# Converting the double-precision weights of a fused attention and MLP kernel a block at a time

## The chip, the cores and the metric

The kernel runs on one core of a Trainium2 chip. Its metric is the device time of one execution in microseconds, from the first to the last of the core's work; lower is better. The kernel before takes 1224.53 us (median of three runs, 1223.8 to 1225.92).

## The reference

Eight batches of eight heads, 576 tokens each, go through causal attention with a decay, and the result through an MLP. Cut to what matters:

```python
# q, k, v: (8, 8, 576, 64) float32, f: (8, 8, 576) float32
scores = q @ k.T / 8 + (cum[:, None] - cum[None, :])      # cum = cumsum(log(clip(f)))
attn = exp(scores - max) / (sum + 1e-9)                   # causal rows
x = (attn @ v), heads side by side                        # (4608, 512)
h = x @ w_in                                              # w_in (512, 2048), float64
g = where(h >= 1, h, where(h <= -1, 0, (h + 1) ** 2 / 4))
out = g @ w_out                                           # w_out (2048, 512), float64
```

Both weight matrices arrive as 64-bit floats, 8 MB each. [...]

## The kernel before, in words

**Attention.** The work is cut into 36 jobs of two heads (a "pair") of one batch; batch 0 is cut into two parts, so that it has eight jobs. A job loads q, k and v, makes scores on PE (L470), the decay with its causal mask on GpSimd, called POOL here (L476, L480), the sum of both with its running minimum on DVE (L559), the exponential on ACT (L563), the normalised weights on ACT and DVE (L577, L583, or a transpose through PE, L490 to L512, in the first five jobs), and the product with v on PE (L532, L603).

**MLP.** Tokens go in chunks of 256, features in eight blocks of 256 (NB = 8). A unit is one chunk and one block: 24 or more matmuls against w_in (L645), three passes on ACT and two on DVE (L654 to L659), twelve matmuls against w_out (L673). Numbers are carried as a high and a low half of 16 bits each, hence three products instead of one. Units are woven between the steps of the attention jobs, as many as have their tokens and their weights.

**Weights.** Block i needs 256 columns of w_in (half-step n = 2i) and 256 rows of w_out (n = 2i + 1). `weight_load` brings the raw words of one half-step as two transfers of 512 KB into two raw places; the list RAW names them. There are 21: the 17 tiles `place0` to `place16` that the halves go to later, and two halves each of `early` and `x1`, two activation buffers that the start leaves free. `weight_split(n)` then works on one half-step, on each of its two parts of 512 elements by itself:

- DVE makes single-precision words by three integer operations (L195, L198, L201; the scratch is the tile `u`, which the MLP units use too);
- a bound of the magnitude is taken per partition: by a maximum on DVE for w_in (L211), by a sum of magnitudes on ACT for w_out (L215, whose elementwise result goes to a place that is not needed yet); L216 joins the two parts;
- `across` makes one number of the 128 partitions by a transpose and a product on PE (L120, L130) with four small DVE operations around them (L122, L123, L127, L131), and `scale_of` a power of two from it by three more (L108, L102, L110);
- ACT writes the high half (L222); POOL (w_in, L224 and L225) or DVE (w_out, L227) writes the low half.

CONVERT says how many half-steps each of the jobs 3 to 7 takes in; after each of them `load_weights` issues further loads, up to AHEAD = 4 half-steps on, as long as their raw place isn't one that waits to be converted.

**Order.** A scheduler sets the order on each engine when the kernel is built, and each engine runs its list strictly in that order. All loads, and the transposes made by DMA from job 5 on, go through one queue, SP. When an instruction waits, everything behind it on its engine or queue waits too.

Of the kernel before, what the change touches and what calls it, by code (L numbers as in the profile page):

```python
# [8 lines left out]
F32 = mybir.dt.float32  # L9
# [6 lines left out]
P = 128  # L16
# [16 lines left out]

EARLY = ((0, 0, 3), (0, 3, 6), (0, 6, 8))

CONVERT = {3: 3, 4: 3, 5: 4, 6: 4, 7: 2}
LOADS = {0: 2, 1: 3, 2: 4}
AHEAD = 4

RAW = (  # L40
    (1, 2), (3, 4), (5, 6), (7, 8), (9, 10), (11, 12), (16, 17), (18, 19),
    (20, 13), (14, 15), (11, 12), (16, 17), (18, 19), (20, 14), (15, 16), (17, 18),
)


@with_exitstack
def kernel(
# [58 lines left out]
    def scale_of(scale, power, m):  # L106

        nc.vector.tensor_scalar(out=power, in0=m, scalar1=1.0 / TOP, scalar2=None, op0=ALU.mult)  # L108
        even_pow2(power, power)
        nc.vector.reciprocal(scale, power)  # L110

    def across(dst, m):

        n = m.shape[1]
        pt = ps.tile([P, 512], F32, name="s")
        nc.tensor.transpose(pt[0:n, 0:P], m, ident)  # L120
# [10 lines left out]
        nc.vector.tensor_copy(dst, pt[:, P:P + n])  # L131
# [33 lines left out]

    place = [const.tile([P, 2, 2 * DM], F16, name=f"place{i}") for i in range(2 * NB + 1)]
    slots = [t.rearrange("p l c -> p (l c)").bitcast(I32) for t in place] + [r.bitcast(I32) for r in (early[:, 2 * DM:4 * DM], early[:, 0:2 * DM], x1[:, 0:2 * DM], x1[:, 2 * DM:4 * DM])]
    wi = [place[2 * i].rearrange("p l (t c) -> p l t c", t=NKT) for i in range(NB)]  # L170
    wo = [place[2 * i + 1].rearrange("p l (t c) -> p l t c", t=2) for i in range(NB)]
    mi = const.tile([P, NB], F32, name="mi")
    mp = const.tile([P, 2, NB], F32, name="mp")
    sw = const.tile([P, 2, NB], F32, name="sw")

    def weight_load(n):
        i, j = divmod(n, 2)
        if j == 0:
            src = w_in.bitcast(I32)[:, i * 4 * P:(i + 1) * 4 * P].rearrange("(t p) c -> p t c", p=P)
        else:  # L180
            src = w_out.bitcast(I32)[i * 2 * P:(i + 1) * 2 * P, :].rearrange("(t p) c -> p t c", p=P)
        n = src.shape[1] // 2
        for k_, slot in enumerate(RAW[2 * i + j]):
            nc.sync.dma_start(
                slots[slot].rearrange("p (t c) -> p t c", t=n), src[:, n * k_:n * (k_ + 1), :]
            )

    def weight_split(n):
        i, j = divmod(n, 2)
        parts = []  # L190
        for k_, slot in enumerate(RAW[n]):
            top = slots[slot][:, 1::2]
            low = slots[slot][:, 0::2]
            bits = two.tile([P, DM], F32, name="u").bitcast(I32)
            nc.vector.tensor_scalar(  # L195
                out=bits, in0=top, scalar1=0x07FFFFFF, scalar2=3, op0=ALU.bitwise_and, op1=ALU.logical_shift_left
            )
            nc.vector.scalar_tensor_tensor(  # L198
                out=bits, in0=low, scalar=29, in1=bits, op0=ALU.logical_shift_right, op1=ALU.bitwise_or
            )  # L200
# [3 lines left out]
            parts.append((top.bitcast(F32), slice(k_ * DM, (k_ + 1) * DM)))
        hi = place[n][:, 0]
        lo = place[n][:, 1]
        m1 = tiny.tile([P, 1], F32, name="m1", bufs=2)
        ms = tiny.tile([P, 2], F32, name="ms", bufs=2)
        for k_, (wf, c) in enumerate(parts):
            if j == 0:  # L210
                nc.vector.tensor_reduce(  # L211
                    out=ms[:, k_:k_ + 1], in_=wf, axis=AX.X, op=ALU.max, apply_absolute_value=True
                )
            else:
                nc.scalar.activation(lo[:, c], wf, AF.Abs, accum_out=ms[:, k_:k_ + 1])  # L215
        nc.vector.tensor_reduce(out=m1, in_=ms, axis=AX.X, op=ALU.max)  # L216
        m = mi[:, i:i + 1] if j == 0 else tiny.tile([P, 1], F32, name="m2")
        across(m, m1)
        s = sw[:, j, i:i + 1]
        scale_of(s, mp[:, j, i:i + 1], m)  # L220
        for wf, c in parts:
            nc.scalar.activation(hi[:, c], wf, AF.Copy, scale=s)  # L222
            if n % 2 == 0:
                nc.gpsimd.tensor_scalar(out=wf, in0=wf, scalar1=s, scalar2=0.0, op0=ALU.mult, op1=ALU.add)  # L224
                nc.gpsimd.tensor_tensor(out=lo[:, c], in0=wf, in1=hi[:, c], op=ALU.subtract)  # L225
# [519 lines left out]
    for p in range(njobs + 1):  # L745
        w = pairs[p] if p < njobs else None
        nxt = pairs[p + 1] if p + 1 < njobs else None
        steps = []
        if w:
            if w.b not in xs:  # L750
                xs[w.b] = xpool.tile([P, NPAIR, 2, S], F16, name="x")
            if p + 2 < njobs:
                pairs.append(load(p + 2))
            if nxt:
                load_decay(nxt, 0)
                prepare(nxt)
            scores(w, w.r0)

            def step(r):
                if r + 1 < w.r1:  # L760
                    scores(w, r + 1)
                if r == w.r1 - 2 and nxt:
                    load_decay(nxt, 1)
                    if nxt.hp == 0 and nxt.r0 == 0:
                        value_scale(nxt.b)
                    split_values(nxt)
                weights(w, r)
                if r == w.r1 - 1 and p + 2 < njobs:
                    measure(pairs[p + 2])

            steps = [lambda r=r: step(r) for r in range(w.r0, w.r1)]
        if p > 0:
            wp = pairs[p - 1]

            def finish():
                nonlocal tokens
                (early_values if wp.p < NPE else values)(wp, xs[wp.b])
                if wp.hp == NPAIR - 1:
                    if wp.b and wp.r0 == 0:
                        join_scales(wp.b - 1)  # L780
                    tokens = wp.b * S + wp.s1

            steps.insert(4 if len(steps) == NT5 else 2, finish)
        load_weights(LOADS.get(p, 0))
        blocks = CONVERT.get(p, 0)
        quota = -(-ready() // (NPAIR - (p + NPAIR - 1) % NPAIR))
        before, wbefore = done, nw
        for i, st in enumerate(steps):
            st()
            while nw - wbefore < blocks * (i + 1) // len(steps):  # L790
                weight_step()
            while ready() and done - before < quota * (i + 1) // len(steps):
# [39 lines left out]
```

## Time and profile before

| | |
|---|---|
| median of three runs | 1224.53 us |
| profiled execution: its time, its span | 1223.2 us, 1221.4 us |
| busy over the span: PE, DVE, ACT, POOL | 92%, 70%, 62%, 36% |
| weight operations: first and last start | 19.5 us (L195), 200.4 us (L227) |
| weight loads on SP | 32 of 512 KB |

The span is cut into stretches below: the weights are converted in the first 215 us, and PE is close to full from 400 us on. A time in a row of groups is the sum of the durations, and durations of neighbouring instructions overlap a little: how far apart two of them start is read from the timeline.

### The profile page before, as it was taken

What the parts mean: (1) busy time and instruction counts of PE and PEld (TensorE: products, weight loads), DVE (VectorE), ACT (ScalarE), POOL (GpSimd) and SP (SyncE); (2) the same over time, 40 slices, a digit from 0 to 9 for tenths busy, and PEclk for the clock granted to TensorE, in tenths of its full rate; (3) what the DMA queues carried; (4) which work ended last, traced back from release to release, by engine and by line L of the source; (5) the groups of instructions that cost most, each with busy time, mean ns of one, the idle gap of its engine ahead of it and who ended that gap; (6) DMA issues with size and microseconds to landing.
All of it is one profiled execution on the core that took longest, in us unless ns stands there. A gap on an engine that the chain in (4) does not pass through costs nothing.

```text
span 1221.4 us, 24896 instructions
## 1 busy us (share of the span) xinstructions
PE 1118.6 (92%) x8865; PEld 683.2 (56%) x8865; DVE 854.6 (70%) x2423; ACT 762.5 (62%) x1558; POOL 443.9 (36%) x695
## 2 busy tenths in 40 slices
PE   5587677996799999999999999989999999999998
PEld 3354334553456565565655665655665566567665
DVE  6889888776877787777666767777877796522222
ACT  3574665774756676757666667666767687644443
POOL 4758644542633254334333224432443263100000
PEclk9878788899699999999999999999999999999999
DMA  8957543768866768657636736666966685300000
GB/s 230 278 149 199 135 123 79 138 126 175 172 129 140 146 131 162 126 120 141 126 88 134 150 69 126 140 138 123 172 123 135 143 154 114 72 24 2 18 19 18
DMA packets 408541, 152.21 MB, mean 125 GB/s; under 512 B 384225, under 2 KB 385249, under 8 KB 408417
## 3 DMA queue, kind: packets, MB, share of 16 engines
q1 hardware_dynamic: 408416, 150.63, 57.7%
q8 instruction: 69, 1.13, 0.4%
q14 instruction: 56, 0.45, 0.1%
HBM read 75.64 MB, written 9.58 MB: 70 GB/s over the span
## 4 chain that ended last, share of the span: by engine, by line
PE 38%; DVE 5%; DMA 3%; issue 2%; SPq 2%; ACT 2%; POOL 0%; DVEq 0%; ACTq 0%
PE ph L645 16%; PE po L673 16%; PE s L470 3%; PE big L603 2%; DMA ck<-in_v_dram 1%; DVE pr L583 1%; DVE sdr L559 1%; SPq L332 1%; DMA qk<-in_k_dram 1%; PE big L470 1%; DMA qk<-in_q_dram 1%; DVE u L656 1%; DVE g L659 1%; SPq L429 0%; ACT pr L577 0%
## 5 line engine op out<-in xcount | busy, mean ns | idle before, releaser
L645 PE MATMUL ph<-x,place 128*128 128x256 f16 (+3 forms) x4608 | 449.9, 250 | 12.6 <-DVE u L656 7.9
L673 PE MATMUL po<-place,g 128*128 128x512 f16 x1728 | 423.7, 384 | 9.4 <-DVE g L659 5.8
L645 PEld LDWEIGHTS <-place 128*128 128x128 f16 x4608 | 356.0, 99 | 115.2 <-issue 44.8
L673 PEld LDWEIGHTS <-g 128*128 128x128 f16 x1728 | 161.3, 99 | 184.8 <-issue 21.1
L476 POOL TENSOR_SCALAR sdr<-ck,nsig,cqs 128x128 f32<-128x128 f32 (+1 forms) x192 | 155.9, 815 | 229.8 <-DVE pr L583 218.1
L563 ACT ACTIVATE sdr<-sdr,nm 128x384 f32<-128x384 f32 (+1 forms) x248 | 138.5, 559 | 95.1 <-DVE nm L559 84.8
L470 PE MATMUL s<-qkT 64*128 64x384 f16 (+6 forms) x704 | 158.9, 359 | 23.3 <-DVE nm L559 21.6
L656 DVE SCALAR_TENSOR_TENSOR u<-ph,z,u 128x512 f32<-128x512 f32 x136 | 101.6, 747 | 108.8 <-ACT u L655 108.2
L654 ACT ACTIVATE u<-ph,z 128x512 f32<-128x512 f32 x136 | 104.7, 769 | 111.3 <-PE ph L645 110.6
L658 ACT ACTIVATE g<-u,z 128x512 f16<-128x512 f32 x136 | 97.7, 718 | 90.8 <-DVE u L656 90.2
L577 ACT ACTIVATE pr<-sdr,rc 128x384 f16<-128x384 f32 (+1 forms) x236 | 120.0, 556 | 38.7 <-DVE rc L574 16.9
L583 DVE SCALAR_TENSOR_TENSOR pr<-sdr,rc,pr 128x384 f16<-128x384 f32 (+2 forms) x232 | 126.3, 573 | 25.4 <-ACT pr L577 24.2
L476 POOL TENSOR_SCALAR sd<-ck,nsig,cqs 64x576 f32<-64x576 f32 x48 | 54.2, 1130 | 242.6 <-ACT qs L403 91.0
L659 DVE SCALAR_TENSOR_TENSOR g<-u,z,g 128x512 f16<-128x512 f32 x136 | 103.6, 761 | 38.4 <-ACT g L658 38.2
L559 DVE CUSTOM_DVE_ANT_0 sdr<-s,sdr,nalpha 128x128 f32<-128x128 f32 (+1 forms) x192 | 103.2, 545 | 23.1 <-PE s L470 17.0
L470 PEld LDWEIGHTS <-qkT 64*128 64x128 f16 (+1 forms) x864 | 47.9, 99 | 88.0 <-issue 66.5
L480 POOL TENSOR_SCALAR_AFFINE_SELECT sdr<-sdr 128x128 f32<-128x128 f32 x248 | 92.2, 381 | 10.9
L655 ACT ACTIVATE u<-u 128x512 f32<-128x512 f32 x144 | 89.8, 623 | 2.5
L603 PE MATMUL big<-pT,vs 128*64 128x320 f16 (+3 forms) x1098 | 72.8, 284 | 0.9 <-DVE nm L559 0.5
L381 DVE TENSOR_REDUCE m2q<-qk 128x1 f32<-128x640 f32 x48 | 39.2, 817 | 44.2 <-DMA qk<-in_q_dram 34.6
L603 PEld LDWEIGHTS <-vs 128*64 128x64 f16 x1098 | 49.9, 112 | 28.8 <-issue 10.1
L476 POOL TENSOR_SCALAR sdr<-ck,cq 128x384 f32<-128x384 f32 (+3 forms) x56 | 41.1, 734 | 62.5 <-DVE pr L583 34.1
(161 smaller groups left out, 1092.7 us busy)
## 6 DMA issues: line engine op xcount, KB each, us to landing
ck<-cum_d SPq DMA_DIRECT2D x64, 288.0 KB, 3.6
out_dram<-ot SPq DMA_DIRECT2D x36, 256.0 KB, 2.6
qk<-in_k_dram SPq DMA_DIRECT2D x64, 128.0 KB, 2.9
ck<-in_v_dram SPq DMA_DIRECT2D x28, 288.0 KB, 2.9
v<-in_v_dram SPq DMA_DIRECT2D x62, 128.0 KB, 2.8
qk<-in_q_dram SPq DMA_DIRECT2D x56, 128.0 KB, 2.7
place<-in_moe_w_in_dram SPq DMA_DIRECT2D x12, 512.0 KB, 5.4
place<-in_moe_w_out_dram SPq DMA_DIRECT2D x10, 512.0 KB, 6.7
```

The costliest lines, as they stand in the source:

```text
L470: nc.tensor.matmul(sds[h % len(sds)][1][p0:p1, c0:c1], lhsT=a[rows, q0 - w.s0:q0 - w.s0 + p1 - p0], rhs=b[rows, c0:c1], start=(i == 0), st ...
L476: nc.gpsimd.tensor_scalar(out=sd[p0:p1, 0:wid], in0=w.ck[h][p0:p1, 0:wid], scalar1=w.nsig if w.p < NQK else w.nsig[p0:p1], scalar2=w.cqs[p ...
L559: nc.vector.tensor_tensor_reduce(out=a, in0=sp[:, 0:wid], in1=a, scale=w.nalpha, scalar=BIG, op0=ALU.add, op1=ALU.min, accum_out=nm[:, i:i ...
L563: nc.scalar.activation(a, a, AF.Exp, bias=nm[:, i:i + 1], scale=-1.0, accum_out=sm[:, i:i + 1])
L577: nc.scalar.activation(pr[:, :, 0, i, :], a, AF.Copy, scale=rc[:, i:i + 1])
L583: nc.vector.scalar_tensor_tensor(out=pr[:, :, 1, i, :], in0=a, scalar=rc[:, i:i + 1], in1=pr[:, :, 0, i, :], op0=ALU.mult, op1=ALU.subtract,)
L603: nc.tensor.matmul(av[64 * h:64 * h + 64, at + s0:at + s1], lhsT=w.vs[:, vl, h, t, :], rhs=w.pT[:, t, pl, h, s0:s1], start=(t == 0 and pi ...
L645: nc.tensor.matmul(ph[:, fi, a0:a1], lhsT=wi[fb][:, wl, t, fi * P:(fi + 1) * P], rhs=xs[b][:, t, xl, s0:s0 + a1 - a0], start=(fi == 0 and ...
L654: nc.scalar.activation(u, h, AF.Relu, scale=z.u[:, i:i + 1], bias=z.h[:, i:i + 1])
L656: nc.vector.scalar_tensor_tensor(out=u, in0=h, scalar=z.t[:, i:i + 1], in1=u, op0=ALU.max, op1=ALU.min)
L659: nc.vector.scalar_tensor_tensor(out=g[:, 1], in0=u, scalar=z.r[:, i:i + 1], in1=g[:, 0], op0=ALU.mult, op1=ALU.subtract)
L673: nc.tensor.matmul(po[ch][i], lhsT=g[:, gl, fi * TC + i * P:fi * TC + (i + 1) * P], rhs=wo[fb][:, wl, fi, :], start=(first and fi == 0 and ...
```

## The change

One step now takes a block, that is both matrices. Each half-step's raw words come by one transfer of 1 MB into 8 KB per partition (two neighbouring places, or the whole of what was two halves of `early` or `x1`); the 17 tiles have become one tile `place`. The three integer operations go over 1024 elements, with a scratch tile `bits` of their own. Both bounds are sums of magnitudes on ACT. `across` and `scale_of` run once per block on two columns, with one more copy (into `mi`). The high half is one ACT pass of 1024, the low half one pass of POOL or DVE. CONVERT counts blocks: 2, 1, 2, 2, 1 (before, in half-steps: 3, 3, 4, 4, 2).

```diff
-CONVERT = {3: 3, 4: 3, 5: 4, 6: 4, 7: 2}
+CONVERT = {3: 2, 4: 1, 5: 2, 6: 2, 7: 1}
-RAW = (
-    (1, 2), (3, 4), (5, 6), (7, 8), (9, 10), (11, 12), (16, 17), (18, 19),
-    (20, 13), (14, 15), (11, 12), (16, 17), (18, 19), (20, 14), (15, 16), (17, 18),
-)
+RAW = (2, 4, 6, 8, 10, 12, 14, "early", 10, 12, 14, "next", "early", 14, "next", "early")
...
-    place = [const.tile([P, 2, 2 * DM], F16, name=f"place{i}") for i in range(2 * NB + 1)]
+    place = const.tile([P, 2 * NB + 1, 2, 2 * DM], F16, name="place")
+    bits = const.tile([P, 2 * DM], I32, name="bits")
...
-        for k_, slot in enumerate(RAW[2 * i + j]):
-            nc.sync.dma_start(
-                slots[slot].rearrange("p (t c) -> p t c", t=n), src[:, n * k_:n * (k_ + 1), :]
-            )
+        nc.sync.dma_start(raw(n).rearrange("p (t c) -> p t c", t=src.shape[1]), src)
-    def weight_split(n):
-        i, j = divmod(n, 2)
+    def weight_split(i):
+        m2 = tiny.tile([P, 2], F32, name="m2w", bufs=2)
+        words = []
+        for j in range(2):
+            n = 2 * i + j
+            top = raw(n)[:, 1::2]
+            low = raw(n)[:, 0::2]
             nc.vector.tensor_scalar(
                 out=bits, in0=top, scalar1=0x07FFFFFF, scalar2=3, op0=ALU.bitwise_and, op1=ALU.logical_shift_left
             )
...
+            words.append(top.bitcast(F32))
+            nc.scalar.activation(place[:, n, 1], words[j], AF.Abs, accum_out=m2[:, j:j + 1])
+        m = tiny.tile([P, 2], F32, name="mw", bufs=2)
+        across(m, m2)
+        nc.vector.tensor_copy(mi[:, i:i + 1], m[:, 0:1])
+        scale_of(sw[:, :, i], mp[:, :, i], m)
+        for j in range(2):
+            n = 2 * i + j
+            hi, lo, s = place[:, n, 0], place[:, n, 1], sw[:, j, i:i + 1]
+            nc.scalar.activation(hi, words[j], AF.Copy, scale=s)
             if j == 0:
-                nc.vector.tensor_reduce(
-                    out=ms[:, k_:k_ + 1], in_=wf, axis=AX.X, op=ALU.max, apply_absolute_value=True
+                nc.gpsimd.tensor_scalar(
+                    out=words[j], in0=words[j], scalar1=s, scalar2=0.0, op0=ALU.mult, op1=ALU.add
                 )
-            else:
-                nc.scalar.activation(lo[:, c], wf, AF.Abs, accum_out=ms[:, k_:k_ + 1])
...
+                nc.gpsimd.tensor_tensor(out=lo, in0=words[j], in1=hi, op=ALU.subtract)
             else:
                 nc.vector.scalar_tensor_tensor(
-                    out=lo[:, c], in0=wf, scalar=s, in1=hi[:, c], op0=ALU.mult, op1=ALU.subtract
+                    out=lo, in0=words[j], scalar=s, in1=hi, op0=ALU.mult, op1=ALU.subtract
                 )
...
     def weight_step():
         nonlocal nw
-        load_weights(nw + 1)
+        load_weights(2 * nw + 2)
         weight_split(nw)
         nw += 1
-        load_weights(nw + AHEAD)
+        load_weights(2 * nw + AHEAD)
```

Lines behind the change are numbered 6 less in the changed kernel (L650 there is L656 here), those just ahead of it 3 less. Three places show what the scheduler makes of it.

DVE, the first weights, between the rows of job 0 (L559 is L553 in the changed kernel). Before:

```order
L195 TENSOR_SCALAR u<-place_91 128x512 [waits DMAHW7_49]
L198 SCALAR_TENSOR_TENSOR u<-place_91,u 128x512 [waits DVE_49]
L559 ISA sdr_120,nm<-s,sdr_120 128x256 [waits PE_49,Pool_49]
L559 ISA nm 128x1
L195 TENSOR_SCALAR u<-place_92 128x512 [waits DMAHW0_49]
L201 SCALAR_TENSOR_TENSOR place_91<-place_91,u 128x512 [waits DVE_49]
```

and after:

```order
L196 TENSOR_SCALAR bits<-place 128x1024 [waits DMAHW7_49]
L560 TENSOR_SCALAR rc<-sm_244 128x2 [waits Activation_49]
L553 ISA pr_114,nm<-s,pr_114 128x128 [waits PE_49,Pool_49]
L553 ISA nm 128x1
L199 SCALAR_TENSOR_TENSOR bits<-place,bits 128x1024 [waits DVE_49]
L561 RECIPROCAL rc<-rc 128x2 [waits DVE_49]
L202 SCALAR_TENSOR_TENSOR place<-place,bits 128x1024 [waits DVE_49]
```

The first operation now waits for 1 MB instead of 512 KB, and each operation covers what two did.

ACT, the end of the first block and the bounds of the next (rows of the first five jobs stand ahead of both). Before:

```order
L222 ACTIVATE place_90<-place_92,sw 128x512 [waits DMAHW0_49]
L512 ACTIVATE pT<-ph 128x4x128 [waits PE_49]
L539 ACTIVATE x<-po_779,sv 128x256 [waits PE_49]
L215 ACTIVATE place_91,ms<-place_93 128x512 [waits DMAHW1_49,Pool_49]
L215 ACTIVATE place_91,ms<-place_94 128x512 [waits DMAHW2_49]
L222 ACTIVATE place_91<-place_93,sw 128x512 [waits DVE_49]
```

and after:

```order
L214 ACTIVATE place<-place,sw 128x1024 [waits DVE_49]
L214 ACTIVATE place<-place,sw 128x1024
L506 ACTIVATE pT<-ph 128x2x128 [waits PE_49]
L506 ACTIVATE pT<-ph 128x4x128 [waits PE_49]
L206 ACTIVATE place,m2w<-place 128x1024 [waits DMAHW1_49,Pool_49]
L206 ACTIVATE place,m2w<-place 128x1024 [waits DMAHW2_49]
L206 ACTIVATE place,m2w<-place 128x1024 [waits DMAHW5_49,DVE_49,Activation_49]
L206 ACTIVATE place,m2w<-place 128x1024 [waits DMAHW6_49,DVE_49]
```

The pass for the bound still waits there for POOL, which reads the raw words that it writes over; behind it stand four such passes in a row now.

SP, the last refills of raw places, between the loads of v for batch 1's scale (L245 before, L239 after) and the decay rows (L343, L337). Before:

```order
L245 DMA ck<-in_v_dram 128x576 [waits DMAHW7_49,DMAHW0_49,DVE_49]
L245 DMA ck<-in_v_dram 128x576 [waits DMAHW1_49,DMAHW0_49,DVE_49]
L184 DMA place_106<-in_moe_w_in_dram 128x2x512 [waits DVE_49]
L184 DMA x<-in_moe_w_out_dram 128x1024 [waits DMAHW3_49,DVE_49]
L343 DMA ck<-cum_d 128x576 [waits DMAHW4_49,DMAHW1_49,DVE_49]
L184 DMA x<-in_moe_w_out_dram 128x1024 [waits DMAHW5_49,Pool_49]
```

and after:

```order
L187 DMA x<-in_moe_w_in_dram 128x4x512 [waits DMAHW0_49,DVE_49]
L187 DMA place<-in_moe_w_out_dram 128x2x1024 [waits DMAHW1_49,Pool_49]
L239 DMA ck<-in_v_dram 128x576 [waits DMAHW3_49,DMAHW2_49,DVE_49]
L239 DMA ck<-in_v_dram 128x576 [waits DMAHW2_49,DVE_49]
L337 DMA ck<-cum_d 128x576 [waits DMAHW4_49,DMAHW3_49,DVE_49]
L187 DMA x<-in_moe_w_out_dram 128x2x1024 [waits DMAHW5_49,Pool_49]
```

Two refills of 1 MB, which wait for DVE and POOL to be done with the raw words of earlier blocks, now stand ahead of the last two loads of v; before, the refills stood behind them.

More of the change, by code (lines that the diff above doesn't have):

```diff
@@ L164, in decay_sums @@
         nc.vector.tensor_copy(cq.rearrange("p t n -> p (t n)"), pt[:, 0:NT5 * nb])
-    place = [const.tile([P, 2, 2 * DM], F16, name=f"place{i}") for i in range(2 * NB + 1)]
-    slots = [t.rearrange("p l c -> p (l c)").bitcast(I32) for t in place] + [r.bitcast(I32) for r in (early[:, 2 * DM:4 * DM], early[:, 0:2 * DM], x1[:, 0:2 * DM], x1[:, 2 * DM:4 * DM])]
-    wi = [place[2 * i].rearrange("p l (t c) -> p l t c", t=NKT) for i in range(NB)]
-    wo = [place[2 * i + 1].rearrange("p l (t c) -> p l t c", t=2) for i in range(NB)]
+    place = const.tile([P, 2 * NB + 1, 2, 2 * DM], F16, name="place")
+    wi = [place[:, 2 * i].rearrange("p l (t c) -> p l t c", t=NKT) for i in range(NB)]
+    wo = [place[:, 2 * i + 1].rearrange("p l (t c) -> p l t c", t=2) for i in range(NB)]
     mi = const.tile([P, NB], F32, name="mi")
@@ L174, with raw @@
     sw = const.tile([P, 2, NB], F32, name="sw")
+    bits = const.tile([P, 2 * DM], I32, name="bits")
+    def raw(n):
+        where = RAW[n]
+        if where == "early":
+            return early.bitcast(I32)[:, 0:4 * DM]
+        if where == "next":
+            return x1.bitcast(I32)[:, 0:4 * DM]
+        return place[:, where:where + 2].rearrange("p n l c -> p (n l c)").bitcast(I32)
     def weight_load(n):
@@ L181, in weight_load @@
             src = w_out.bitcast(I32)[i * 2 * P:(i + 1) * 2 * P, :].rearrange("(t p) c -> p t c", p=P)
-        n = src.shape[1] // 2
-        for k_, slot in enumerate(RAW[2 * i + j]):
-            nc.sync.dma_start(
-                slots[slot].rearrange("p (t c) -> p t c", t=n), src[:, n * k_:n * (k_ + 1), :]
-            )
-    def weight_split(n):
-        i, j = divmod(n, 2)
[L190 to L194, printed above, removed]
+        nc.sync.dma_start(raw(n).rearrange("p (t c) -> p t c", t=src.shape[1]), src)
[6 more added lines that the diff above has]
+            low = raw(n)[:, 0::2]
             nc.vector.tensor_scalar(
@@ L203, in weight_split @@
             )
[L204 to L209, printed above, removed]
+            words.append(top.bitcast(F32))
[8 more added lines that the diff above has]
+            nc.scalar.activation(hi, words[j], AF.Copy, scale=s)
             if j == 0:
-                nc.vector.tensor_reduce(
-                    out=ms[:, k_:k_ + 1], in_=wf, axis=AX.X, op=ALU.max, apply_absolute_value=True
-                )
-            else:
[L215 to L225, printed above, removed]
+                nc.gpsimd.tensor_scalar(
+                    out=words[j], in0=words[j], scalar1=s, scalar2=0.0, op0=ALU.mult, op1=ALU.add
+                )
+                nc.gpsimd.tensor_tensor(out=lo, in0=words[j], in1=hi, op=ALU.subtract)
             else:
                 nc.vector.scalar_tensor_tensor(
-                    out=lo[:, c], in0=wf, scalar=s, in1=hi[:, c], op0=ALU.mult, op1=ALU.subtract
+                    out=lo, in0=words[j], scalar=s, in1=hi, op0=ALU.mult, op1=ALU.subtract
                 )
@@ L718, in load_weights @@
         nonlocal nload
-        while nload < min(n, 2 * NB) and not any(set(RAW[nload]) & set(r) for r in RAW[nw:nload]):
+        while nload < min(n, 2 * NB) and RAW[nload] not in RAW[2 * nw:nload]:
             weight_load(nload)
@@ L724, in weight_step @@
         nonlocal nw
-        load_weights(nw + 1)
+        load_weights(2 * nw + 2)
         weight_split(nw)
         nw += 1
-        load_weights(nw + AHEAD)
+        load_weights(2 * nw + AHEAD)
         for first, end in groups:
-            if nw == 2 * end:
+            if nw == end:
                 z = moe_scales(0, first, end - 1, True)
@@ L792 @@
             while ready() and done - before < quota * (i + 1) // len(steps):
-                if units[done] not in bsc and nw < 2 * NB:
+                if units[done] not in bsc and nw < NB:
                     break
```

## The prediction

> **What bounds the kernel now.** I read the busy time by stretches first: where PE is full, only its own work counts.
>
> ```profile
> core 0: us, PE busy (x) PEld busy (x) DVE busy (x) ACT busy (x) POOL busy (x), PEclk, DMA share, GB/s
> 0.00:215.00 215.00, 151.74 (x791) 86.74 (x791) 177.11 (x562) 125.41 (x285) 123.57 (x166) 0.83 0.63 171
> 215.00:400.00 185.00, 165.33 (x1289) 95.54 (x1290) 137.96 (x404) 121.70 (x262) 78.02 (x133) 0.91 0.72 147
> 400.00:600.00 200.00, 191.10 (x1721) 118.24 (x1719) 153.27 (x448) 135.26 (x279) 78.94 (x130) 0.99 0.67 134
> 600.00:800.00 200.00, 199.42 (x1530) 120.31 (x1527) 140.49 (x387) 131.77 (x262) 65.48 (x106) 1.00 0.61 120
> ...
> sum 1221.40, PE 1118.56 PEld 683.16 DVE 854.58 ACT 762.51 POOL 443.88; mean PE 186.43 PEld 113.86 DVE 142.43 ACT 127.09 POOL 73.98
> ```
>
> From 400 us on PE is busy 96% and more, in a fixed order; whatever is won earlier arrives at the end as it is. In the first 215 us, where the weights are converted, PE has 63 us of idleness. There DVE leads, as the same view cut finer shows:
>
> ```profile
> 20.00:50.00 30.00, 24.03 (x133) 15.74 (x131) 25.27 (x85) 18.96 (x60) 17.09 (x29) 1.00 0.96 277
> 50.00:90.00 40.00, 25.10 (x108) 14.50 (x109) 31.71 (x113) 23.35 (x57) 24.47 (x30) 0.66 0.68 192
> 90.00:150.00 60.00, 42.04 (x251) 24.39 (x249) 56.21 (x141) 35.40 (x66) 44.17 (x40) 0.80 0.64 161
> 150.00:215.00 65.00, 51.04 (x273) 26.31 (x270) 54.19 (x201) 39.98 (x86) 28.54 (x40) 0.84 0.43 107
> ```
>
> DVE is busy 167 of these 195 us, 86%, and 94% from 90 to 150. The transfers are at their limit only up to 50 us (share 0.96). So the change is worth what it takes off DVE here, less what it makes DVE wait.
>
> **What DVE is spared.** DVE starts an instruction before the last one's record ends, so I price by the distance of starts. Four neighbours of the timeline, and a chain in which each needs the one before:
>
> ```profile
> 24.77 0.69 DVE L198 SCALAR_TENSOR_TENSOR u<-place,u 128x512 int32<-128x512 int32 x1
> 25.38 0.69 DVE L211 TENSOR_REDUCE ms<-place 128x1 f32<-128x512 f32 x1
> 25.98 0.48 DVE L195 TENSOR_SCALAR u<-place 128x512 int32<-128x512 int32 x1
> 26.38 0.28 DVE L559 CUSTOM_DVE_ANT_0 pr<-s,pr 128x128 f32<-128x128 f32 x1
> ...
> 62.19 0.15 DVE L108 TENSOR_SCALAR mp<-m 128x1 f32<-128x1 f32 x1
> 62.26 0.15 DVE L131 COPY mi<-s 128x1 f32<-128x1 f32 x1
> 62.38 0.15 DVE L102 TENSOR_SCALAR mp<-mp 128x1 int32<-128x1 int32 x1
> ```
>
> A two-input operation of 512 takes 0.61 us of DVE, a reduction 0.60, the first bit operation 0.40; a small one 0.07, or 0.19 where it needs its neighbour (L108 to L102).
> For 1024 elements the trace has no row; the slope comes from one operation at two widths, beside the groups removed or merged:
>
> ```profile
> L583 DVE SCALAR_TENSOR_TENSOR pr<-sdr,rc,pr 128x512 f16<-128x512 f32 x62 | 44.4, 746 | 6.9 <-ACT pr L577 6.8
> L583 DVE SCALAR_TENSOR_TENSOR pr<-sdr,rc,pr 128x128 f16<-128x128 f32 x56 | 18.4, 359 | 4.9 <-ACT pr L577 4.8
> L211 DVE TENSOR_REDUCE ms<-place 128x1 f32<-128x512 f32 x12 | 7.9, 676 | 0.0
> L211 DVE TENSOR_REDUCE ms<-x 128x1 f32<-128x512 f32 x4 | 2.6, 668 | 0.0
> L216 DVE TENSOR_REDUCE m<-ms 128x1 f32<-128x2 f32 x16 | 2.0, 143 | 7.0 <-ACT place L215 7.0
> ```
>
> (746 - 359) / 384 = 1.01 ns per element, so 512 more cost 0.52 us, and a two-input operation of 1024 takes 1.13. The first bit operation lies between 0.66 (half that slope) and 0.80 (twice the present one); I take 0.68, since its 0.40 for 512 allows no full slope.
>
> - Bit operations: per half-step 2 x (0.40 + 0.61 + 0.61) = 3.24 now, 0.68 + 2 x 1.13 = 2.94 then; 16 half-steps save 4.8 us (2.9 to 5.1).
> - L211, 16 reductions of 0.60: 9.6 us.
> - L216, 16 of 0.07 to 0.14: 1.6 us (1.1 to 2.2).
> - `across` and `scale_of`, seven small operations once per block, eight times fewer, at 0.07 to 0.19: 3.9 to 10.6 us, less 0.6 to 1.5 for the new copy. I take 5.
> - Low half of w_out: 2 x 0.61 becomes 1.13; eight times 0.09 is 0.7 us.
>
> Together 21.7 us (16.6 to 27.6).
>
> **What else moves.** ACT takes the bounds of w_in.
>
> ```profile
> L222 ACT ACTIVATE place<-place,sw 128x512 f16<-128x512 f32 x22 | 15.4, 751 | 14.2 <-DVE sw L110 11.8 <-DVE mp L102 2.4
> L215 ACT ACTIVATE place<-place 128x512 f16<-128x512 f32 x10 | 6.5, 658 | 12.2 <-POOL place L225 11.8 <-issue 0.3
> L215 ACT ACTIVATION_READ_ACCUMULATOR place<-place 128x1 f32 x10 | 1.9, 194 | 0.0
> L577 ACT ACTIVATE pr<-sdr,rc 128x512 f16<-128x512 f32 x62 | 41.3, 712 | 17.9 <-DVE rc L574 8.7 <-issue 6.6 <-ACT sdr L563 1.9
> L577 ACT ACTIVATE pr<-sdr,rc 128x128 f16<-128x128 f32 x56 | 19.1, 388 | 1.1 <-ACT sdr L563 0.5 <-DMA pT<-pr 0.4 <-DVE rc L574 0.3
> ```
>
> ACT's slope is (712 - 388) / 384 = 0.84 ns. Now 32 x 0.751 + 16 x 0.852 = 37.7 us; then 16 x 1.18 for the high halves and 16 x 1.28 for the bounds, 39.5 us. The 1.8 us more lie in ACT's 90 us of idleness: nothing, and 1.8 without that cover. But ACT waits 11.8 us in two places for POOL, and the pass that waits stays, now at each block. I leave that wait as it is.
>
> POOL's two passes become half as many, at most twice as long (L225 below): no loss.
>
> ```profile
> L225 POOL TENSOR_TENSOR place<-place,place 128x512 f16<-128x512 f32 x12 | 14.5, 1221 | 0.1
> L224 POOL TENSOR_SCALAR place<-place,sw 128x512 f32<-128x512 f32 x12 | 10.7, 892 | 3.3 <-ACT place L222 2.8
> ```
>
> **What becomes late.** Two things. The first bit operation waits for 1 MB where it waited for 512 KB: at 277 GB/s half a megabyte more is 1.9 us, between 0 (rows of job 0 run meanwhile) and 1.9; I take 1.5. And raw places are refilled in pieces of twice the size, later in the order.
>
> ```profile
>   DVE u L195: 5.2, 6
> ...
> DMA to landing us min/median/max: 3.1/5.7/8.7
> ```
>
> These are who waits for the weight loads, and how long a load takes. DVE waits 5.2 us in all; with pieces of twice the size I take twice that, 5.2 us more. The bounds: nothing, since there are half as many; and four refills (blocks 4 to 7) that nothing covers, each 1.2 us of ACT, 2 x (0.892 + 1.221) = 4.2 us of POOL and 5.7 + 1.9 = 7.6 us of transfer, 13 us, so 52 in all. Behind a bit operation that waits stand the attention rows of its job.
>
> Sum: -21.7 + 1.5 + 5.2 = -15.0 us of DVE. DVE is what ends last for 86% of this time; 0.86 x 15.0 = 12.9 us reach the end. 1223.2 - 12.9 = 1210.3 for the profiled execution; its 1223.2 stand 1.3 below the median, so 1211.6 as a median.
>
> [...]
>
> ```profile
> L198 DVE SCALAR_TENSOR_TENSOR u<-place,u x22: 665/692/1636, 20.1 to 165.5; 128x512 int32<-128x512 int32 x22
> L198 DVE SCALAR_TENSOR_TENSOR u<-place,u 128x512 int32<-128x512 int32 x22 | 18.2, 827 | 0.2
> ```
>
> The mean is 135 ns above the median, and the longest 0.94 above it: some are held up, 3 us in this group. [...]
>
> **Rivals.** *Refills decide; slower.* Blocks 4 to 7 get their raw words into places that POOL and DVE must first be done with, and SP then holds the loads of v and the decay rows behind two such transfers. For it: in the order there are only some ten DVE rows between the release and the next need. Against it: the 5.2 us above, for places reused in the same manner. Of the 52 us it must expose more than 21.7 - 1.5 = 20 to make a loss; at 60%, 31, it loses 31 - 20 = 11 us: 1224.5 + 11 = 1236.
>
> *Won and lost again; no change.* Between 215 and 400 us PE idles 20 us, and there DVE waits for loads of v that stand behind transposes on SP. Were that stretch paced by the queue alone, the start would only arrive earlier at the same wait: 1224. Against it: those transposes are issued when the jobs reach them, so they move along.
>
> *PE recovers too; faster than I say.* The granted clock is 0.66 from 50 to 90 us, behind a PE wait of ten:
>
> ```profile
> 57.64 0.58 PE L120 MATMUL s<-ident,m 128*1 128x128 f32 x2 [10.43 <-DVE m L216]
> ```
>
> With half the detours through `across` these waits could halve and the clock stay up: at clock 1.0 PE's 25.1 us of that stretch would shrink by a third, 8.5 us. With all of DVE's 21.7 - 1.5 = 20.2 us reaching the end, that makes 28.7 us: 1224.5 - 28.7 = 1196. [...] Against it: that wait was for POOL behind ACT, and it stays.
>
> **How the numbers follow.** My forecast (1200 to 1222) 0.53; PE recovers (below 1200) 0.12; no change 0.14; refills (above 1227) 0.21. A measurement tells 0.2%, 2.4 us. Faster 0.65, same 0.14, slower 0.21. The range leaves a tenth out on each side: down to 1195, up to 1232, into the refill case.
>
> **What would show it.** L211 and L216 gone; two-input bit operations near 1.2 us; DVE's busy time 20 to 30 us less; the last low half of w_out (200.4 us now) some 13 us earlier, and the stretch from 400 us on unchanged in length. Wrong: DVE waiting for weight loads by more than 20 us, or the conversion ending earlier and the end not.

## The result, and the profile after

| | before | after |
|---|---|---|
| median | 1224.66 us (four runs, 1223.8 to 1225.92) | 1212.3 us (four runs, 1210.65 to 1213.42) |
| ratio, 95% interval | | 0.9897 (0.988 to 0.9914) |
| profiled execution's span | 1221.4 us | 1211.0 us |

The change saves 12.4 us, 1.0%. The forecast was 1211.6. But the trace does not show the way that the forecast took. The busy time by stretches of the changed kernel, with the columns of before:

```profile
0.00:215.00 215.00, 157.20 (x754) 88.50 (x755) 157.20 (x423) 128.28 (x266) 112.79 (x147) 0.79 0.64 169
215.00:400.00 185.00, 169.74 (x1365) 98.92 (x1364) 144.44 (x422) 126.32 (x275) 81.49 (x140) 0.94 0.74 152
400.00:600.00 200.00, 193.64 (x1749) 120.50 (x1748) 152.91 (x443) 134.20 (x275) 75.36 (x124) 0.99 0.69 138
...
20.00:50.00 30.00, 25.75 (x125) 16.49 (x123) 21.38 (x63) 22.21 (x64) 15.78 (x28) 1.00 0.89 260
50.00:90.00 40.00, 26.87 (x118) 15.37 (x119) 34.63 (x77) 24.89 (x52) 29.24 (x28) 0.70 0.78 227
90.00:150.00 60.00, 41.92 (x226) 22.72 (x224) 41.05 (x93) 36.16 (x60) 35.54 (x33) 0.77 0.59 130
150.00:215.00 65.00, 53.27 (x258) 28.27 (x258) 50.57 (x163) 37.41 (x76) 23.11 (x31) 0.71 0.45 119
```

DVE's busy time from 20 to 215 us is 147.6 us (the third column of the last four rows) where it was 167.4: the 20 us are spared. PE is busy 5.5 us more up to 215, but at a granted clock of 0.79 in place of 0.83. To see how far the program has come, I take one landmark per job, the row in which ACT writes its result x. The first two rows are before (job 8, the last of batch 0, and job 15), the next two after, each from the timeline of its kernel:

```profile
214.03 0.41 ACT L612 ACTIVATE x<-big 128x320 f16<-128x320 f32 x1
411.20 0.63 ACT L612 ACTIVATE x<-big 128x576 f16<-128x576 f32 x1
```

```profile
213.40 0.41 ACT L606 ACTIVATE x<-big 128x320 f16<-128x320 f32 x1
400.95 0.63 ACT L606 ACTIVATE x<-big 128x576 f16<-128x576 f32 x1
```

Job 8, near the end of the conversion, is written 0.6 us earlier, and the last low half of w_out starts at 199.40 in place of 200.36 us. From job 8 to job 15 the changed kernel takes 187.5 us where the one before takes 197.2. From there to the end both take the same, 810.1 and 810.2. So by these landmarks the time is won after the conversion, in a stretch whose operations the change does not touch, while the 20 us spared on DVE have come to nothing. The experiments are about these two halves.

### The profile page after: what moved, and what is told of

It is laid out like the page before. It is cut to its first block, busy times and chain, and to the rows that moved or that the text cites. A ratio compares the mean times of both kernels' runs of the same rounds, so it can differ in the third digit from the quotient of the medians.

```text
span 1211.0 us, 24642 instructions
## 1 busy us (share of the span) xinstructions
PE 1121.7 (93%) x8841; PEld 684.2 (56%) x8841; DVE 838.4 (69%) x2287; ACT 766.0 (63%) x1542; POOL 432.9 (36%) x679
## 3 DMA queue, kind: packets, MB, share of 16 engines
q8 instruction: 69, 1.13, 0.4%
## 4 chain that ended last, share of the span: by engine, by line
PE 55%; DVE 8%; DMA 5%; issue 3%; ACT 3%; SPq 3%; POOL 1%; DVEq 0%; POOLq 0%; ACTq 0%
PE ph L639 22%; PE po L667 22%; PE s L464 5%; PE big L597 3%; DMA ck<-in_v_dram 2%; DVE pr L577 2%; DMA qk<-in_q_dram 2%; PE big L464 1%; DVE sdr L553 1%; SPq L326 1%; DVE g L653 1%; DVE u L650 1%; ACT pr L571 1%; DMA ck<-cum_d 1%; PE s L127 1%
## 5 line engine op out<-in xcount | busy, mean ns | idle before, releaser
L667 PE MATMUL po<-place,g 128*128 128x512 f16 x1728 | 418.6, 381 | 10.6 <-ACT g L652 6.0
L470 POOL TENSOR_SCALAR sdr<-ck,nsig,cqs 128x128 f32<-128x128 f32 (+1 forms) x192 | 155.1, 810 | 215.1 <-DVE pr L577 208.1
L557 ACT ACTIVATE sdr<-sdr,nm 128x384 f32<-128x384 f32 (+1 forms) x248 | 138.6, 559 | 108.0 <-DVE nm L553 94.7
L464 PE MATMUL s<-qkT 64*128 64x384 f16 (+6 forms) x704 | 168.4, 365 | 15.5 <-DVE nm L553 14.6
L650 DVE SCALAR_TENSOR_TENSOR u<-ph,z,u 128x512 f32<-128x512 f32 x136 | 101.5, 746 | 106.0 <-ACT u L649 105.6
L648 ACT ACTIVATE u<-ph,z 128x512 f32<-128x512 f32 x136 | 104.7, 770 | 108.0 <-PE ph L639 107.4
L470 POOL TENSOR_SCALAR sd<-ck,nsig,cqs 64x576 f32<-64x576 f32 x48 | 51.2, 1066 | 248.7 <-DMA ck<-cum_d 91.4
L577 DVE SCALAR_TENSOR_TENSOR pr<-sdr,rc,pr 128x384 f16<-128x384 f32 (+2 forms) x232 | 127.7, 580 | 14.8 <-ACT pr L571 12.6
L553 DVE CUSTOM_DVE_ANT_0 sdr<-s,sdr,nalpha 128x128 f32<-128x128 f32 (+1 forms) x192 | 103.3, 545 | 28.7 <-PE s L464 22.0
L474 POOL TENSOR_SCALAR_AFFINE_SELECT sdr<-sdr 128x128 f32<-128x128 f32 x248 | 91.7, 380 | 10.9
L470 POOL TENSOR_SCALAR sdr<-ck,cq 128x384 f32<-128x384 f32 (+3 forms) x56 | 46.0, 821 | 49.0 <-DVE pr L577 21.1
```

What stands on the lines that cost most here:

```text
L464: nc.tensor.matmul(sds[h % len(sds)][1][p0:p1, c0:c1], lhsT=a[rows, q0 - w.s0:q0 - w.s0 + p1 - p0], rhs=b[rows, c0:c1], start=(i == 0), st ...
L470: nc.gpsimd.tensor_scalar(out=sd[p0:p1, 0:wid], in0=w.ck[h][p0:p1, 0:wid], scalar1=w.nsig if w.p < NQK else w.nsig[p0:p1], scalar2=w.cqs[p ...
L553: nc.vector.tensor_tensor_reduce(out=a, in0=sp[:, 0:wid], in1=a, scale=w.nalpha, scalar=BIG, op0=ALU.add, op1=ALU.min, accum_out=nm[:, i:i ...
L557: nc.scalar.activation(a, a, AF.Exp, bias=nm[:, i:i + 1], scale=-1.0, accum_out=sm[:, i:i + 1])
L577: nc.vector.scalar_tensor_tensor(out=pr[:, :, 1, i, :], in0=a, scalar=rc[:, i:i + 1], in1=pr[:, :, 0, i, :], op0=ALU.mult, op1=ALU.subtract,)
L648: nc.scalar.activation(u, h, AF.Relu, scale=z.u[:, i:i + 1], bias=z.h[:, i:i + 1])
```

## The experiments

Theory A is the prediction's: what DVE is spared up to 215 us reaches the end, 0.86 us for each. The rivals: B, that something in the change itself costs in the first stage what DVE is spared; C, that the gain is one of pace; D, that it is won at the loads of v after the conversion. The kernels ran on several chips, whose medians of the kernel before differ by 3 us, so the ratios are compared and not the medians. This table gives the landmarks of all profiles in us; the sections below refer to it.

| kernel | job 8 | job 8 to 12 | job 12 to 15 | job 15 to end | median, ratio to before (95%) |
|---|---|---|---|---|---|
| before, and a second profile | 214.0, 215.1 | 104.9, 104.5 | 92.3, 89.1 | 810.2, 812.1 | 1224.66 |
| after, and a second profile | 213.4, 212.8 | 101.1, 102.0 | 86.4, 87.1 | 810.1, 811.7 | 1212.3, 0.9897 (0.988 to 0.9914) |
| after, second bit operation twice | 230.7 | 107.1 | 85.7 | 811.3 | 1235.5, 1.0081 (1.0051 to 1.0112) |
| after, without it | 208.6 | 103.5 | 85.7 | 811.1 | 1205.91, 0.9849 (0.9813 to 0.9885) |
| after, two scales, and a second profile | 203.8, 204.2 | 105.7, 104.6 | 84.1, 86.3 | 807.3, 806.8 | 1204.73, 0.9821 (0.9774 to 0.9867) |
| after, bound of w_in on DVE | 210.2 | 104.8 | 86.6 | 811.0 | 1214.38, 0.9895 (0.9851 to 0.9939) |
| after, loads of 512 KB | 213.4 | 106.5 | 88.6 | 806.6 | 1217.97, 0.9947 (0.9927 to 0.9966) |
| after, four buffers for v and decay rows | 218.4 | 101.4 | 85.5 | 807.7 | 1215.63, 0.991 (0.9881 to 0.9939) |
| before, joint step alone | 220.5 | 108.0 | 88.3 | 808.7 | 1223.61, 0.9996 (0.9975 to 1.0016) |
| before, pace of the change | 223.5 | 108.0 | 84.3 | 818.8 | 1227.16, 1.0021 (0.999 to 1.0051) |
| before, four buffers | 210.0 | 99.0 | 85.7 | 808.1 | 1204.69, 0.9812 (0.9766 to 0.9858) |

Ratios are to runs of the kernel before on the same chip. A kernel's profiles give job 8 within 1.1 us of each other; the expectations below call it the ninth write, since ACT writes x once ahead of the jobs, and job 15 the sixteenth.

### More and less work on DVE

The first kernel adds

```diff
             nc.vector.scalar_tensor_tensor(
                 out=bits, in0=low, scalar=29, in1=bits, op0=ALU.logical_shift_right, op1=ALU.bitwise_or
             )
+            nc.vector.scalar_tensor_tensor(
+                out=bits, in0=low, scalar=29, in1=bits, op0=ALU.logical_shift_right, op1=ALU.bitwise_or
+            )
```

and the second takes both away.

> The changed kernel with the second bit operation (the two-input one over 1024 elements, 1.22 us median) done twice in each of the 16 half-steps; the second time changes nothing in the words. DVE gets 16 x 1.22 = 19.5 us more to do in the conversion, about what the change spared it; PE's order of work stays nearly as it is. Theory A (what DVE is spared in the first 215 us reaches the end, 0.86 of it): 1212.3 + 0.86 x 19.5 = 1229. Theory B (jobs are no earlier at 215 us although DVE has 20 us less to do, so DVE's time there is not what the end hangs on): within 3 us of 1212.

> The changed kernel without the second bit operation: the lowest three bits of each word's fraction are left out. DVE has 16 x 1.22 = 19.5 us less to do in the conversion. Theory A: 1212.3 - 0.86 x 19.5 = 1195.5. Theory B: within 3 us of 1212. A mixture (DVE was the bound in before, and another engine is by now) would show as e_twice slower and this one unchanged.

With 19.5 us more on DVE, job 8 comes 17.3 us later, 0.89 per us, and the end 0.0184 x 1224.7 = 22.5 us later: more than was added, since job 8 to 12 takes 5 to 6 us longer as well, where this edit adds nothing. With 19.5 us less (the words then lack their lowest three bits) job 8 comes 4.8 us earlier, 0.25 per us, and the end 5.9 us. At job 8 theory A holds for what is added, and for a quarter of what is taken away. The quarter is uncertain: the interval of 0.9849 just touches the changed kernel's, and the profiled execution, 1210.8 us, is the longest of four with a median of 1205.9. This fits the mixture, a kernel in which DVE has just stopped being the bound and something else stands at the same height; what stands there, these two runs do not say.

### The joint step

```diff
-        m2 = tiny.tile([P, 2], F32, name="m2w", bufs=2)
...
-            nc.scalar.activation(place[:, n, 1], words[j], AF.Abs, accum_out=m2[:, j:j + 1])
-        m = tiny.tile([P, 2], F32, name="mw", bufs=2)
-        across(m, m2)
-        nc.vector.tensor_copy(mi[:, i:i + 1], m[:, 0:1])
-        scale_of(sw[:, :, i], mp[:, :, i], m)
-        for j in range(2):
-            n = 2 * i + j
+            m1 = tiny.tile([P, 1], F32, name="m1", bufs=2)
+            nc.scalar.activation(place[:, n, 1], words[j], AF.Abs, accum_out=m1)
+            m = mi[:, i:i + 1] if j == 0 else tiny.tile([P, 1], F32, name="m2")
+            across(m, m1)
+            scale_of(sw[:, j, i:i + 1], mp[:, j, i:i + 1], m)
```

> The changed kernel with the scales of the two matrices found one after the other, each by its own transposition and product, as before (16 times in place of 8). Theory A (DVE's time carries): the prediction put this part at 5 us of DVE (3.9 to 10.6), so 1212.3 + 0.86 x 5 = 1217 (1216 to 1221). Theory B (the joint step costs what it spares, since no weight can be scaled before the slower of two bounds is there; PE stands 14.8 us and POOL 31.8 us in such waits in the first 215 us): those waits shrink and the time falls, 1200 to 1210.

Faster, by 0.0076 x 1224.7 = 9 us against the changed kernel, as theory B has it. Job 8 comes at 203.8, and again in a second profile (its label has a buffer in it that the kernel does not have):

> The changed kernel with two scales once more, for a second profile. If the earlier end of the first stage is of the program, the ninth job's result is written at 202 to 206 us again (203.8 in the first profile, 213.4 in the changed kernel); if it was one execution's luck, nearer to 213.

So with two scales the first stage is 10 us shorter than before: there the time spared on DVE does arrive. Where it went in the changed kernel is seen in DVE's own waits from 10 to 235 us. Their rows add up to 36.6 us before, 55.3 after and 39.6 with two scales (36.0, 55.5 and 39.4 in the second profiles). So the changed kernel's DVE works 20 us less and waits 19 us more, and with two scales this waiting is nearly gone. The weight loads, shown further below, are one part of it. The other rows that grew most, before, after and with two scales (engine, line, waited for: us in total, times, longest):

```profile
DVE sdr L559 <- PE s L470: 2.3, 4, 1.1
DVE m L246 <- DMA ck<-in_v_dram: 3.0, 4, 0.8
```

```profile
DVE sdr L553 <- PE s L464: 13.6, 11, 5.7
DVE m L240 <- DMA ck<-in_v_dram: 6.1, 3, 4.8
```

```profile
DVE sdr L550 <- PE s L461: 3.8, 5, 1.4
DVE m L237 <- DMA ck<-in_v_dram: 2.1, 1, 2.1
```

DVE stands for the attention scores that PE makes, and for loads of v. What PE and POOL stood for from 20 to 215 us, after first, then with two scales:

```profile
PE s L117 <- ACT place L206: 14.8, 4, 8.0
PE ph L639 <- DVE u L650: 9.8, 2, 9.2
...
POOL x L216 <- ACT place L214: 31.8, 2, 28.8
```

```profile
PE s L117 <- ACT place L206: 9.2, 3, 7.9
...
POOL x L213 <- ACT place L211: 6.2, 1, 6.2
POOL place L213 <- ACT place L211: 2.8, 2, 1.4
```

PE waits 14.8 us for the bounds and 9.2 with two scales (before it was 14.8 too), and POOL's first pass over w_in stands 35 us behind the high halves (31.8, and 3.6 in a row not shown) where it stands 9, and 5.5 before. The longest of these waits, followed through the timelines of the changed kernel's queue and engines:

```profile
150.91 0.54 SPq L187 DMA_DIRECT2D x<-in_moe_w_in_dram  x1
151.54 0.46 SPq L187 DMA_DIRECT2D place<-in_moe_w_out_dram  x1
...
159.83 0.69 DVE L196 TENSOR_SCALAR bits<-place 128x1024 int32<-128x1024 int32 x1 [5.32 <-DMA place<-in_moe_w_out_dram]
...
164.15 0.68 DVE L196 TENSOR_SCALAR bits<-x 128x1024 int32<-128x1024 int32 x1
...
168.45 1.21 DVE L202 SCALAR_TENSOR_TENSOR x<-x,bits 128x1024 int32<-128x1024 int32 x1
...
174.42 0.17 DVE L107 RECIPROCAL sw<-mp 128x2 f32<-128x2 f32 x1
...
174.62 1.20 ACT L214 ACTIVATE place<-x,sw 128x1024 f16<-128x1024 f32 x1
...
175.93 1.19 POOL L216 TENSOR_SCALAR x<-x,sw 128x1024 f32<-128x1024 f32 x1 [28.76 <-ACT place L214]
```

The refill issued at 151.54 is this block's w_out (the one at 150.91 is w_in of the next block, whose bits start at 164.15). The block's own w_in left at 110.55, its bits start at 134.59 and its bound at 139.18, but its scale comes with that of w_out, at 174.42, and only then do ACT's high half and POOL's pass start, at 174.62 and 175.93. POOL has stood since 147 us, and the decay rows of the attention jobs are queued behind this pass. That this standing of POOL costs time by itself is not shown: DVE waits no longer for POOL's decay rows (5.7 us, L474) than with two scales (9.0, L471). What can be followed is the refills: the last one takes the place of this w_in and leaves at 179.37 us, as POOL's low half from there ends (177.21 + 2.13), so its bits start at 184.4 us where with two scales the last bits start at 159.8; and DVE waits more for weight loads. The rows on who sat idle before the first bit operation, for before (L195), after (L196) and after with two scales (L195):

```profile
  DMA place<-in_moe_w_in_dram: 3.7, 5
  DMA x<-in_moe_w_out_dram: 1.5, 1
```

```profile
  DMA place<-in_moe_w_out_dram: 5.8, 2
  DMA place<-in_moe_w_in_dram: 5.5, 3
```

```profile
  DMA place<-in_moe_w_in_dram: 3.7, 4
  DMA place<-in_moe_w_out_dram: 0.8, 1
```

5.2, 11.3 and 4.5 us, and 4.6, 12.1 and 4.8 in the second profiles. The kernel with 4.5 loads 1 MB at a time too: the doubling comes from the joint step, not from the size of the pieces. Then the joint step without the rest, put into the kernel before (the raw places and the pace of the change come with it; cut to what matters):

```diff
-CONVERT = {3: 3, 4: 3, 5: 4, 6: 4, 7: 2}
+CONVERT = {3: 2, 4: 1, 5: 2, 6: 2, 7: 1}
...
+            nc.vector.tensor_reduce(out=m2[:, j:j + 1], in_=ms, axis=AX.X, op=ALU.max)
+        across(m, m2)
+        nc.vector.tensor_copy(mi[:, i:i + 1], m[:, 0:1])
+        scale_of(sw[:, :, i], mp[:, :, i], m)
...
```

> The kernel before with the joint step alone: both matrices of a block in one step, one transposition and one product for both bounds, the raw places as in the change (in pieces of 512 KB), everything else as before, the reductions on DVE and the halves of 512 among it. Theory A: DVE is spared about 5 us (3.9 to 10.6), 1224.5 - 0.86 x 5 = 1220. Theory B (the step costs more by its waits than it spares; taking it out of the changed kernel made that 7.6 us faster): 1228 to 1233, and the ninth job ends its product later than at 214 us.

Its profile shows the same marks, though it is of one of the three long executions among ten (1227.3 us, median 1223.6): DVE waits 14.2 us for weight loads (9.7 and 4.5) in place of 5.2, PE's waits from 20 to 215 us are 63.6 us in all where two profiles of before have 52.1 and 50.6, and job 8 comes at 220.5, 6 us later. (The 63.6 is the sum of PE's rows in the waits.) But its time does not differ from before's measurably (0.9996, 0.9975 to 1.0016); the profiled execution (span 1225.5) is 4.1 us behind at the end. Nor does the late job 8 prove the joint step: the kernel before with nothing but the pace of the change, shown below, writes it at 223.5 us, again in a long execution. It waits only 2.3 us for weight loads, so the longer wait for weights is seen from both sides. The loss at job 8 and at the end is shown only from the side of the changed kernel, and theory B's 1228 to 1233 was too much.

### The bound on ACT, the pieces of the loads, the pace

```diff
-            nc.scalar.activation(place[:, n, 1], words[j], AF.Abs, accum_out=m2[:, j:j + 1])
+            if j == 0:
+                nc.vector.tensor_reduce(
+                    out=m2[:, 0:1], in_=words[j], axis=AX.X, op=ALU.max, apply_absolute_value=True
+                )
+            else:
+                nc.scalar.activation(place[:, n, 1], words[j], AF.Abs, accum_out=m2[:, j:j + 1])
```

> The changed kernel with the bound of w_in a maximum on DVE again, over 1024 elements at once. DVE gets 8 reductions more, each about 0.60 + 0.52 = 1.12 us (an estimate from the rows of the kernel before), 9 us. Theory A: 1212.3 + 0.86 x 9 = 1220. Theory B (in the first 215 us PE waits 14.8 us for the bounds, which are all ACT's now, and ACT for POOL and DVE): shorter waits for ACT make up for it, 1207 to 1213.

The reductions are there, 1.21 us each:

```profile
L207 DVE TENSOR_REDUCE m2w<-place 128x1 f32<-128x1024 f32 x6 | 7.3, 1211 | 0.0
L207 DVE TENSOR_REDUCE m2w<-x 128x1 f32<-128x1024 f32 x2 | 2.4, 1200 | 0.0
```

DVE has 9.7 us more to do, its waits from 10 to 235 us fall from 55.3 to 45.3, and job 8 comes 3 us earlier; the ratio is the changed kernel's (0.9895 and 0.9897). ACT's sum for w_in was worth nothing in the changed kernel, as B has it.

```diff
-        nc.sync.dma_start(raw(n).rearrange("p (t c) -> p t c", t=src.shape[1]), src)
+        h = src.shape[1] // 2
+        r = raw(n).rearrange("p (t c) -> p t c", t=src.shape[1])
+        for k in range(2):
+            nc.sync.dma_start(r[:, h * k:h * (k + 1), :], src[:, h * k:h * (k + 1), :])
```

> The changed kernel with each load of 1 MB made as two of 512 KB, as before. DVE waits 11.3 us for weight loads in the changed kernel and 5.2 us in the one before. Theory A: the 6 us come back, 0.86 x 6 = 5: 1207. Theory B: no change, 1212, DVE's waits there falling all the same.

Neither theory has it: 6 us slower. DVE's wait for weights does not fall (12.8 us, rows of 6.7, 4.8 and 1.3), and job 8 comes at 213.4 as without the edit. The 6 us arise between jobs 8 and 15, where no weights are loaded. They may belong to the order in which the scheduler then puts the rest, which was not tested, and say nothing on the size of pieces.

```diff
-CONVERT = {3: 3, 4: 3, 5: 4, 6: 4, 7: 2}
+CONVERT = {3: 4, 4: 2, 5: 4, 6: 4, 7: 2}
```

> The kernel before, with the half-steps spread over the jobs as the change spreads its blocks: 4, 2, 4, 4, 2 in place of 3, 3, 4, 4, 2. Theory A: DVE has the same to do, no change, 1224.5. Theory C (the gain is one of the order, that is when the blocks are ready for the units): some of the 12 us, 1213 to 1220.

No change (1.0021, 0.999 to 1.0051), which is against C. This kernel's runs spread from 1221.8 to 1237.7 us, and its profile is of a long one.

### After the conversion: the loads of v

> The kernel before, unchanged, for a second profile. In the first one the ninth job's result is written at 214.0 us and the sixteenth's 197 us later; in the changed kernel at 213.4 and 187.5 later. If both stages are of the program: 212 to 216, and 194 to 200 later. If the second difference was one execution's chance: under 192.

> The changed kernel, unchanged, for a second profile: if the stages are of the program, the ninth job's result at 211 to 216 us and the sixteenth's 185 to 190 us later.

Second profiles give job 8 at 215.1 and 212.8, and 193.6 and 189.1 us from there to job 15. The difference of this stretch is 9.7 us in the first pair and 4.5 in the second, 7 in the mean: it has the same sign in both pairs, and its size is known within a few us. (The second profiled executions, 1222.6 and 1215.4 us, lie 7 us apart, the medians 12.4.)

```diff
-                st = two.tile([P, S], F32, name="ck", bufs=3)
+                st = two.tile([P, S], F32, name="ck", bufs=4)
```

The same stands in `load_decay`, which shares these buffers.

> The kernel before with four in place of three buffers for the rows of v whose bound is taken and the rows of decay sums. In the kernel before DVE waits 7.9 us for rows of v between 281 and 319 us, in the changed one 2.6 us between 284 and 314, and it is there that the two part. Theory D (part of the 12 us is won at these loads, not in the conversion): 4 to 8 us less, 1216 to 1221. Theory A: at most 2 us less, 1223 to 1225.

> The changed kernel with the same fourth buffer. Theory D: what is to be had there is had already, so within 3 us of 1212. Theory A: the same small gain as in the kernel before, if any, 1210 to 1212. Were both kernels to gain 4 us and more, the loads of v would be a stall that the change has nothing to do with.

The kernel before gains 23 us (0.9812 x 1227.9 is 1204.8, against 1227.9 on that chip), the changed one nothing. That is D in kind, and three to six times its size. Part of how it works shows on the queue. The four loads of v whose bound batch 2 needs, in before, after, and before with four buffers:

```profile
277.35 0.39 SPq L245 DMA_DIRECT2D ck<-in_v_dram  x1
...
293.62 0.34 SPq L245 DMA_DIRECT2D ck<-in_v_dram  x1
```

```profile
273.79 0.40 SPq L239 DMA_DIRECT2D ck<-in_v_dram  x1
...
288.50 1.00 SPq L239 DMA_DIRECT2D ck<-in_v_dram  x1
```

```profile
271.39 1.02 SPq L245 DMA_DIRECT2D ck<-in_v_dram  x2
...
278.27 0.53 SPq L245 DMA_DIRECT2D ck<-in_v_dram  x1
```

With three buffers each further load waits for one to come free, with transposes between them: 15 to 17 us from first to last, with four buffers 7. Job 12 is written 25.3 to 28.5 us after the fourth load in all twelve profiles with three buffers (25.3 before: 318.9 - 293.6; 26.0 after: 314.5 - 288.5). This fits that these loads pace the program between jobs 8 and 12, and four buffers shorten this stretch by 5.7 us in the kernel before (104.7 to 99.0). In the changed kernel the first of the four leaves 60.4 us after job 8 (273.8 - 213.4) where before it was 63.3, and the four take 1.6 us less (0.5 in the second profiles). Of the 7 us, about 3 are won between jobs 8 and 12 (3.8 and 2.5 in the two pairs). That the places which the scheduler gave these rows are the reason is argued and not shown. With four buffers the fourth load leaves 68 (before) and 70 us (after) after job 8 and job 12 follows 31 us later in both: something else seems to pace there, and the changed kernel gains nothing more.

The other 4 us arise from job 12 to 15, where the two profiles of before take 92.3 and 89.1 us and all twelve others, the re-paced kernel before among them, 84.1 to 88.6. Why before alone is long there is not settled; nor is the rest of the 18 us that the fourth buffer saves it in the profiles (4 to 5 up to job 8, 5 from job 12 to 15, 3 after job 15).

Two kernels beat both: the one before with four buffers (1204.69 us), and the changed one with two scales (1204.73). Both edits together were not run.

## Why the prediction was right in its number and wrong in its path

- **DVE spared, 21.7 us (16.6 to 27.6).** Right. Busy time fell by 20 us up to 215. The wide operations are near what they were priced at by the distance of starts (1.15 us here, 1.13 in the forecast):

```profile
160.55 1.23 DVE L199 SCALAR_TENSOR_TENSOR bits<-place,bits 128x1024 int32<-128x1024 int32 x1
161.70 0.75 DVE L240 TENSOR_REDUCE m<-ck 128x1 f32<-128x576 f32 x1
```

- **`across` and `scale_of` once per block, 5 us spared.** This is the step that failed. I counted seven small instructions per step and left the waits as they were ("no loss" for POOL; "I leave that wait as it is" for ACT). Shared scales make all that follows a scale wait for the later of two matrices: undoing it brings job 8 forward by 9 us and the end by 9, and takes 16 us out of DVE's waits. Without this step, and with waits for weight loads no longer than before, the rest of the sum, 0.86 x (21.7 - 5 - 1.5) = 13 us, is near the 10.5 us by which job 8 comes earlier with two scales than before.
- **DVE waits for weight loads, 5.2 us doubled.** 11.3 us, so the amount was right, and the cause wrong: not pieces of twice the size (loads took 6.8 us in the median where they took 5.7), but refills that leave later in the joint step. It is the refill rival at an eighth of its price (6.1 us more, of 52).
- **The factor 0.86.** Around the changed kernel it held upwards (0.89 per us at job 8) and not downwards (0.25, from one long execution). The forecast took a share of busy time for the share in which DVE ends last. Here that came near for added work; what less work is worth ended at the next chain.
- **The high halves, ACT's bounds: hidden.** Right for ACT's time; but putting reductions back on DVE cost nothing in the changed kernel, where I put 9.6 us on all of L211.
- **From 400 us on unchanged.** Right: 810.1 and 810.2 us from job 15 to the end.
- **13 us earlier at the last low half.** Wrong, 1.0 us. The sign that I had named was "the conversion ending earlier and the end not"; what came is the reverse, an end that is earlier and a conversion that is not, and I had not named that.
- **Rivals.** *Won and lost again* had the place: the stretch of the loads of v between 215 and 400 us matters. But it gave time instead of taking it. *PE recovers* did not happen in the first stage, where the clock went from 0.83 to 0.79; from 215 to 400 it went from 0.91 to 0.94, with PE busy 4.4 us more. That the clock stays up when PE stands less was assumed and is not shown: from 150 to 215 us PE is busy 2.2 us more than before (53.27 and 51.04), at a clock of 0.71 in place of 0.84.
- **Two-input operations held up.** The longest low half of w_out is 1.84 us above the median, where the longest excess of before (L198) was 0.94. This low half ran from 51.3 us, beside a POOL pass of 2.96 us that began at 50.4.

```profile
L221 DVE SCALAR_TENSOR_TENSOR place<-place,sw x5: 1264/1286/3125, 51.3 to 178.1; 128x1024 f16<-128x1024 f32 x5
```

  In sum the holds did not grow: mean above median, times the count, is 4.9 us for L199, L202 and L221, and 6.8 for L198, L201 and L227 before. In both kernels an operation of these lines with no POOL pass beside it is at most 9 ns above its line's median, and the five of the changed kernel that are over 0.4 us above it all ran beside one. But of the 23 that ran beside one for over 0.3 us, 16 are less than 50 ns above the median, and the one-input L196 was held up too (1385 ns at 128.4 us, median 693). What decides which of them is held up, and for how long, is not shown.

That the number was met is thus luck: an error of about 10 us in the joint step, and a gain of about 7 us in a stretch from which I expected none.

## What to carry to other kernels

When two chains are joined so that a step need be done only once, count who waits for the later of the two, not the instructions saved: here the engine that was spared 20 us of work waited 19 us longer, and giving up the joint step took 16 us of that waiting away. Before crediting an engine's saving, look for the chain that stands just below it: here added work cost nearly in full at the next landmark, and removed work paid a quarter. And an edit in one stage changes what the scheduler does in the next: compare landmarks stage by stage, with a second profile, before a gain is put down to the edit.

## What the runs showed of the hardware that was not expected

How long a weight load took from issue to landing, in the changed kernel:

```profile
DMA to landing us min/median/max: 4.8/6.8/13.3
```

1 MB took 6.8 us in the median, 512 KB in the kernel before 5.7, and with the loads split, two behind each other, 5.0 to 6.8 in the medians of the four groups: half the size won about 1 us on this queue.

The wide operations, in the rows of the changed kernel's lines:

```profile
L199 DVE SCALAR_TENSOR_TENSOR bits<-place,bits x11: 1204/1219/2062, 22.1 to 160.6; 128x1024 int32<-128x1024 int32 x11
...
L196 DVE TENSOR_SCALAR bits<-place x11: 672/693/754, 21.3 to 159.8; 128x1024 int32<-128x1024 int32 x11
```

A two-input operation took 1219 ns in the median where 512 elements took 692 (L198 before). If the rest grows with the elements, 165 ns of each are a fixed part (2 x 692 - 1219), an estimate from these two medians. The words are read with a stride of two (a 64-bit weight is a pair of 32-bit words), and the slope, 1.03 ns per element, is still that of L583 (1.01), which reads words side by side. The one-input operation takes 693 ns where 512 elements took 426 (L195 before), 0.52 ns per element and half of the two-input one's 1.03.
